# Up-projection by Strassen's products in the later batches, with weight parts kept in DRAM

## The chip, the cores and the metric

The kernel runs on one core of a Trainium2 chip. What counts is the device time of one execution in microseconds; lower is better. The kernel before takes 679.81 us, the median of three runs (679.27 to 683.58). The engines are named as in the profile: PE is TensorE (matmuls; PEld is its weight load), DVE is VectorE, ACT is ScalarE, POOL is GpSimd, and SP is SyncE, whose queue issues every DMA of this kernel in the order in which they are written.

## What is computed

For each of four batches: an attention with eight heads of 64 channels over 768 tokens, where each query sees a band of 31 keys and 24 block summaries, and then a block on the result x (768 tokens x 512 channels).

```python
scores_l = scale * q @ k.T, masked to |i - j| < 16
scores_s = scale * q @ k_sum.T + log(32)      # k_sum: maximum of each block of 32 keys
a = softmax over both
x = a @ [v, v_sum]                            # v_sum: mean of each block of 32 values
...
h = xt @ U @ V                                # mixes the 768 tokens, rank 32
u = x + h.transpose(0, 2, 1)
ch = np.maximum(u @ w_ch1, 0.0) @ w_ch2       # 512 -> 2048 -> 512
out = u + ch
```

U, V and both weights come as 64-bit floats, everything else in 32 bits.

## The kernel before

**Numbers.** A product of two 32-bit matrices is made of three fast matmuls: each operand is split into a high part (rounded) and a low part (the rest), and high x high, high x low and low x high are added in PSUM. `split` makes the parts: ACT rounds, DVE or POOL subtracts.

**The block on x.** `mix_t`, `mix_s` and `mix_u` compute u with channels on the partitions; `mix_u` (L507) puts three transposes of x and one matmul of the mixing into one PSUM bank, and `mix_u_out` splits the result into uh and ul. `up(st, hf, f)` (L567) makes a piece: 128 hidden channels f (16 of them) for one half hf of the tokens (384), as 12 matmuls with the weights loaded into the array and 384 tokens streaming. `up_out` applies the ReLU and splits into gh and gl (ACT L586, DVE L587). `down` (L590) adds a piece to four PSUM accumulators, one for each 128 output channels, 12 matmuls of 384 columns. `down_rows` (L603) does the same with the gates loaded and 512 weight columns streaming, 9 matmuls for a half of the tokens, and leaves tokens on the partitions.

**The first batch.** Its attention is written out by hand in `START`. A loop over f with both halves inside follows (16 columns, each with four places numbered 4f to 4f+3), since the weights are converted in it: `load_weight` brings 512 KB of 64-bit words, `scale_f64` (ACT), `turn_weights` (POOL and DVE) and `split_weights` (ACT and POOL) make the parts. All 32 tiles of parts stay in SBUF for the rest of the kernel. The loads run up to seven columns ahead. The places 13 to 57 also hold the 28 steps of the second batch's attention (`places`). The rows that `down_rows` leaves are turned by 24 transposes (`turn_rows`, L648).

**The later batches.** A list of 32 pieces a batch, first one half of the tokens, then the other: `up` of a piece, `down` of the piece before it, and one step of the next batch's attention (`later_step`). `finish` adds the result to u (held in `outs`) and stores it.

**Order.** Every engine executes its instructions in the order in which they are written, and waits on semaphores in between. The attention of a head goes: `scores` (PE L290), `exponentials` (DVE L310, ACT L320), `turn_squares` (DVE L340, then a store of 384 KB to DRAM), `fetch_squares` (four loads), `square_values` (PE L389), `normalise` (DVE L401 to L403). `key_maxima` (DVE L255, L272) needs the loaded keys, `value_summaries` (ACT L276) writes rows beside the loaded values.

## Time and profile before

| | |
|---|---|
| median of three runs | 679.81 us |
| the profiled execution's own time | 680.63 us |
| its span on the core | 678.8 us |
| mean granted TensorE clock | 0.997 |
| DMA traffic | 78.31 MB, read 61.73 and written 15.73 in HBM |
| largest group of matmuls | L573 (up), 225.4 us busy for uh, 110.6 us for ul |
| second | L595 (down), 210.3 us and 128.3 us |

A row of a group gives the line, engine, operation and tiles, the count after x, the busy time and the mean length of one in ns, and the idle time of the engine ahead of it with what ended that. Matmuls overlap in the array, so the mean length of a matmul is longer than the interval at which they follow each other. Starts in the timeline show that interval.

### The profile page before, as it was taken

How to read it: one execution, taken by the hardware profiler on the slowest of the kernel's cores; microseconds unless marked ns; L12 is line 12 of the kernel's file. 1: busy time of each engine (PE TensorE's matmuls, PEld its weight loads, DVE VectorE, ACT ScalarE, POOL GpSimd, SP SyncE). 2: the span in 40 equal slices, each digit the busy share in tenths (PEclk: the TensorE clock that was granted, in tenths of full speed). 3: DMA queues.
4: the chain of work that ended last, by engine and by line, in shares of the span. 5: the costliest groups of instructions: out<-in, count | busy, mean ns of one | idle time of the engine just before them, and what ended most of it. 6: DMA issues, size and time to landing. Idle time of an engine off the chain costs nothing.

```text
span 678.8 us, 13070 instructions
## 1 busy us (share of the span) xinstructions
PE 655.2 (97%) x5148; PEld 625.4 (92%) x5148; DVE 303.0 (45%) x947; ACT 216.9 (32%) x511; POOL 199.2 (29%) x292
## 2 busy tenths in 40 slices
PE   5889989999999999999999999999999999999997
PEld 4778868888888999999999999999999999999997
DVE  3677687776755544344321444445431221111112
ACT  3855354554622332223321132333321121111110
POOL 5745956955658222100005003020020120000000
PEclk9999998999999999999999999999999999999999
DMA  9999757783252254334234144335210010001001
GB/s 240 239 327 350 248 164 221 224 224 96 74 134 66 97 151 139 112 113 149 66 112 96 46 108 129 113 112 159 79 60 22 8 40 1 1 1 46 1 1 47
DMA packets 65597, 78.31 MB, mean 115 GB/s; under 512 B 5888, under 2 KB 53888, under 8 KB 65536
## 3 DMA queue, kind: packets, MB, share of 16 engines
q1 hardware_dynamic: 65536, 77.49, 39.3%
q8 instruction: 40, 0.66, 0.4%
q14 instruction: 21, 0.17, 0.1%
HBM read 61.73 MB, written 15.73 MB: 114 GB/s over the span
## 4 chain that ended last, share of the span: by engine, by line
PE 78%; POOL 1%; DMA 1%; DVE 1%; SPq 1%; issue 0%; ACT 0%; DVEq 0%
PE ps_h L573 34%; PE acc L595 29%; PE acc L609 5%; PE ps_s L290 4%; PE ps_x L389 3%; PE ps_u L511 1%; DMA at<-there 1%; PE ps_m L477 1%; PE ps_u L519 1%; POOL val L139 0%; PE ps_o L648 0%; PE ps_r L495 0%; POOL ws L164 0%; DVE o L630 0%; DVE squares L340 0%
## 5 line engine op out<-in xcount | busy, mean ns | idle before, releaser
L573 PE MATMUL ps_h<-uh,ws 128*128 128x384 f32 x1024 | 225.4, 341 | 1.4 <-DVE gl L587 1.4
L595 PE MATMUL acc<-gh,ws 128*128 128x384 f32 x768 | 210.3, 334 | 0.0
L573 PEld LDWEIGHTS ps_h<-uh,ws 128*128 128x128 f32 x1024 | 179.4, 189 | 5.9 <-DVE gl L587 2.0
L587 DVE SCALAR_TENSOR_TENSOR gl<-ps_h,gh 128x384 fp32r<-128x384 f32 x128 | 71.3, 557 | 247.0 <-ACT gh L586 246.8
L586 ACT ACTIVATE gh<-ps_h 128x384 fp32r<-128x384 f32 x128 | 63.0, 492 | 273.3 <-PE ps_h L573 273.2
L595 PEld LDWEIGHTS acc<-gh,ws 128*128 128x128 f32 x768 | 140.0, 188 | 0.0
L595 PE MATMUL acc<-gl,ws 128*128 128x384 f32 x384 | 128.3, 334 | 0.0
L573 PE MATMUL ps_h<-ul,ws 128*128 128x384 f32 x512 | 110.6, 336 | 0.5 <-DVE ul L532 0.5
L320 ACT ACTIVATE e<-e,neg 128x120 f32<-128x120 f32 x192 | 61.8, 388 | 111.0 <-DVE neg L310 108.6
L573 PEld LDWEIGHTS ps_h<-ul,ws 128*128 128x128 f32 x512 | 91.7, 189 | 1.3 <-DVE ul L532 1.3
L595 PEld LDWEIGHTS acc<-gl,ws 128*128 128x128 f32 x384 | 72.1, 188 | 0.0
L310 DVE CUSTOM_DVE_ANT_0 e<-ps_s,mask_sb 128x120 f32<-128x120 f32 x192 | 43.8, 279 | 51.8 <-PE ps_s L290 50.8
L609 PE MATMUL acc<-ws,gh 128*128 128x512 f32 x192 | 66.6, 401 | 0.0
L139 POOL TENSOR_SCALAR val<-raw 128x512 f32<-128x512 f32 x29 | 47.8, 1666 | 31.9 <-ACT raw L126 30.4
L305 POOL MEMSET e<- 128x8 f32 x24 | 2.5, 105 | 183.2 <-DVE squares L340 183.1
L623 POOL TENSOR_TENSOR o<-uh,ul 128x384 f32<-128x384 f32 x32 | 32.5, 1041 | 56.4 <-DVE ul L532 48.2
L164 POOL TENSOR_TENSOR ws<-val,ws 128x512 fp32r<-128x512 f32 x29 | 38.7, 1356 | 25.9 <-ACT ws L163 20.9
L230 POOL TENSOR_TENSOR stage<-stage 128x256 f32<-128x256 f32 (+1 forms) x48 | 30.8, 641 | 46.4 <-DMA stage<-in_vn 44.6
L609 PEld LDWEIGHTS acc<-ws,gh 128*128 128x128 f32 x192 | 35.9, 188 | 7.8 <-POOL ws L164 0.5
L290 PEld LDWEIGHTS ps_s<-kt,qz 128*128 128x128 f32 x288 | 38.8, 191 | 2.3 <-DVE kt L272 1.5
L290 PE MATMUL ps_s<-kt,qz 128*128 128x120 f32 x288 | 39.7, 274 | 1.0 <-DVE kt L272 1.0
L609 PE MATMUL acc<-ws,gl 128*128 128x512 f32 x96 | 37.8, 393 | 0.0
(78 smaller groups left out, 557.4 us busy)
## 6 DMA issues: line engine op xcount, KB each, us to landing
raw<-in_w SPq DMA_DIRECT2D x32, 512.0 KB, 7.7
there<-squares SPq DMA_DIRECT2D x24, 384.0 KB, 2.6
at<-there SPq DMA_DIRECT2D x96, 96.0 KB, 2.6
vt<-in_v SPq DMA_DIRECT2D x48, 146.2 KB, 3.6
kt<-in_k SPq DMA_DIRECT2D x24, 288.0 KB, 4.1
stage<-in_vn SPq DMA_DIRECT2D x24, 256.0 KB, 4.6
out_t<-o SPq DMA_DIRECT2D x32, 192.0 KB, 2.0
qz<-in_q SPq DMA_DIRECT2D x28, 128.0 KB, 4.4
```

Of the source, the lines that this page charges most:

```text
L139: nc.gpsimd.tensor_scalar(f32(bits), f32(hi), 0.0, None, ALU.mult)
L164: engine.tensor_tensor(lo, val, f32(hi), ALU.subtract)
L230: nc.gpsimd.tensor_tensor(t[:, :n], t[:, :n], t[:, n : 2 * n], ALU.add)
L290: nc.tensor.matmul(ps[:, i * KC : (i + 1) * KC], qt[:, 64 + j * P : 64 + j * P + P], kt[:, k0 : k0 + KC], start=True, stop=True,)
L310: nc.vector.tensor_tensor_reduce(out=e[:, i, :], in0=ps[:, i * KC : (i + 1) * KC], in1=mask_sb[:, m, :], scale=-SCALE, scalar=BIG, op0=ALU ...
L320: nc.scalar.activation(e[:, i, :], e[:, i, :], AF.Exp, bias=st.neg[h][:, u : u + 1], scale=-1.0,)
L573: nc.tensor.matmul(ps[:, :NH], w_split[0, f][:, part_w, c * P : (c + 1) * P], ut[:, c, :], start=(n == 0), stop=(n == 3 * NC - 1),)
L586: nc.scalar.activation(gh, ps[:, :NH], AF.Relu)
L587: nc.vector.scalar_tensor_tensor(gl, ps[:, :NH], 0.0, f32(gh), ALU.max, ALU.subtract)
L595: nc.tensor.matmul(acc[c][:, :NH], w_split[1, f][:, part_w, sl], gt, start=(first and j == 0), stop=(last and j == 2),)
L609: nc.tensor.matmul(acc[t], gt[:, sl], w_split[1, f][:, part_w], start=(first and j == 0), stop=(last and j == 2),)
L623: nc.gpsimd.tensor_tensor(o, f32(uh)[:, c, :], f32(ul)[:, c, :], ALU.add)
```

## The change

**Up.** In batches 1 to 3 the up-projection of a whole batch is computed by Strassen's scheme. The matrices are cut in two by two: the tokens into halves, the channels c into even and odd chunks of 128, the hidden channels f into pairs. For each of eight pairs p seven products are computed instead of eight. `product` is 6 matmuls of 384 columns (three of parts, two chunks). Two PSUM accumulators, x and y, take several products each, and ACT and DVE carry intermediate sums into a hidden tile in SBUF (`up_phase`). The weight operands are A11, A12, A22 and four sums S1 to S4; the token operands are B11, B21, B22 and four differences T1 to T4 (`operands`).

**Down.** A second phase goes through the 16 hidden tiles by rows: 18 matmuls of 512 columns each, into six accumulators, with the gates of the next tile made ahead (`gates`). The mixing is added to x in rows (`mix_rows`), and the output of a batch is turned by `finish` at the start of the next one; that of the last batch comes at the end.

**Weights.** SBUF now keeps a ring of five places for each weight matrix. In the first batch the parts of both weights are stored to DRAM (`store_weight`), the sums S1 to S4 are made, split and stored (`sum_weights`, `store_sums`), and raw loads run up to four columns ahead. From then on each tile is fetched from DRAM in the order of its use, four tiles for a pair and one for a column of down, into the ten places (`fetch_weight`; `tick` issues a fetch some steps after a place is given back).

**Steps.** The next batch's attention and mixing is now a list of 46 steps (`later_steps`), in the places 13 to 61 of the first batch and 15 of them in the up phase and 31 in the down phase of a later one. A head's squares are sent one step after they are turned, fetched a head later and used two steps after that.

```diff
-    def borrow(i, f):
-        return wt.tile([P, 2 * DM], F32, name="borrowed", tag=f"w{i}_{f}")
+    def weight_place(i, f, dt=F32):
+        return wt.tile([P, 2 * DM], dt, name="place", tag=f"w{i}_{f % RING}")
...
+        if a == 0:
+            if 1 <= h <= H:
+                send_squares(st, h - 1)
+            if 2 <= h <= H + 1:
+                fetch_squares(st, h - 2)
+            if h < H:
+                scores(st, h, 0)
+                exponentials(st, h, 0)
+            if 3 <= h <= H:
+                load_v(st, h - 1)
+        elif a == 1:
+            if h < H:
+                scores(st, h, 1)
+                exponentials(st, h, 1)
+            if h + 1 < H:
                 key_maxima(st, h + 1)
+            if 1 <= h <= H:
+                for t in range(2):
+                    value_summaries(st, h - 1, t, nc.scalar.copy)
+        else:
+            if h + 2 < H:
                 load_qk(st, h + 2)
...
+            if 2 <= h <= H + 1:
+                square_values(st, h - 2)
+                normalise(st, h - 2)
+            if h < H:
+                turn_squares(st, h)
...
+    def mix_rows(st, i, k):
...
+        x = st.x[:, 2 * k : 2 * k + 2, i * 2 * P : (i + 1) * 2 * P]
+        nc.vector.tensor_tensor(x, x, ps.rearrange("p (j c) -> p j c", j=2), ALU.add)
...
+    def operands(st, i, k):
...
+        ps = turn_tokens(st, k < 2, 2 * i + k % 2)
...
+        elif k == 2:
+            part("B11", ps)
+            st.tmp["T2"] = tmp()
+            nc.vector.tensor_tensor(st.tmp["T1"], st.tmp["T1"], ps, ALU.subtract)
+            nc.vector.tensor_tensor(st.tmp["T2"], st.tmp["T3"], ps, ALU.add)
+            part("T1", st.tmp["T1"])
+            part("T2", st.tmp["T2"])
...
+    def sum_weights(p, n):
...
+        if n == 0:
+            nc.vector.tensor_tensor(raw[:, 1], a2[:, 0], a2[:, 1], ALU.add)
+            nc.vector.tensor_tensor(raw[:, 0], raw[:, 1], a1[:, 0], ALU.subtract)
+        else:
+            nc.vector.tensor_tensor(raw[:, 0], a1[:, 0], a2[:, 0], ALU.subtract)
+            nc.vector.tensor_tensor(raw[:, 1], a1[:, 1], w_sums[p, 0][:, 0], ALU.subtract)
...
+        for b in range(2):
+            split(parts[:, b, 0], parts[:, b, 1], raw[:, b], nc.vector if b else nc.gpsimd)
...
+    def fetch_weight():
+        if len(fetched) < len(stream):
+            key = stream[len(fetched)]
+            there = w_there[key]
+            t = weight_place(*first_places[len(fetched) % (2 * RING)], F32R)[:, : there.shape[-1]]
+            nc.sync.dma_start(out=f32(t), in_=there)
...
+    def traffic(f, i):
+        if i == 0:
+            if 0 < f and f + RING - 1 < NF:
+                load_weight(0, f + RING - 1)
+            if f > NF - RING:
+                fetch_weight()
+        if i == 1 and f > 0:
+            store_weight(1, f - 1)
...
+            store_weight(0, f)
+        if i == 3 and f > 0:
+            store_sums((f - 1) // 2, (f - 1) % 2)
...
+        for p in range(NF // 2):
...
+            a11, a12 = use_weight("A", p)
+            x = half_bank("ps_h")
+            product(x, a11, op["B11"], first=True)
+            nc.scalar.copy(c[:, 0, 0], x)
+            yield
+            y = half_bank("ps_h")
+            product(y, a12, op["B21"], first=True)
+            nc.vector.tensor_tensor(c[:, 0, 0], c[:, 0, 0], y, ALU.add)
+            free_place()
+            yield
+            if prev:
+                third(*prev)
+                yield
+            s2, s1 = use_weight("S0", p)
+            product(x, s2, op["T2"])
+            nc.scalar.copy(c[:, 0, 1], x)
+            yield
+            if prev:
+                second(*prev)
+                yield
+            y = half_bank("ps_h")
+            product(y, s1, op["T1"], first=True)
+            free_place()
+            yield
+            s3, s4 = use_weight("S1", p)
+            (a22,) = use_weight("D", p)
+            product(x, s3, op["T3"])
...
+            nc.scalar.copy(c[:, 1, 1], x)
+            nc.vector.tensor_tensor(c[:, 1, 1], c[:, 1, 1], y, ALU.add)
...
+    def down_phase(st, g):
...
+            w = use_weight("down", f)
+            ahead = gates(st, f + 1) if f + 1 < NF else None
...
+    def finish(st, hf, c):
+        ps = turn_tokens(st, hf, c)
+        o = mo.tile([P, DM], F32, name="o", tag="val", bufs=8)[:, :NH]
+        nc.scalar.copy(o, ps)
...
-    pieces = [(b, hf, f, hf * NF + f) for b in range(1, B) for hf in range(2) for f in range(NF)]
...
-            g = up_out(up(cur, hf, f))
...
-            down(acc, pf, pg, pf == 0, pf == NF - 1)
...
+    UP, DOWN = 7 * NF // 2 - 2, NF * NU
+    FIRST_STEPS = 15
...
+        steps = spread(mine, 4, UP)
...
+        steps = spread(theirs, 0, DOWN - 5)
```

How the order of instructions moves shows at three places. First the SP queue in the first batch's loop, where the second batch's attention runs. Before: L540 is a raw weight load, L205 and L206 values, L350 the squares' fetch, L342 their store, L184 to L191 keys and queries.

```order
L205 DMA vt<-in_v 96x390
L206 DMA vt<-in_v 96x390
L350 DMA at<-there 32x4x192 x4
L342 DMA there<-squares 128x768
L184 DMA kt<-in_k 128x3x192
L190 DMA qz_84<-in_q 64x3x128
L191 DMA qz_84<-in_q 64x4x128
L540 DMA raw_1653<-in_w 128x1024
L540 DMA raw_1655<-in_w 128x1024
```

After (L638 raw load, L698 store of parts, L227 and L228 values, L375 fetch, L367 store of squares, L206 to L213 keys and queries):

```order
L367 DMA there<-squares 128x768
L375 DMA at<-there 32x4x192 x4
L227 DMA vt<-in_v 96x390
L228 DMA vt<-in_v 96x390
L638 DMA place<-in_w 128x1024
L698 DMA weight<-place 128x1024 x2
L206 DMA kt<-in_k 128x3x192
L212 DMA qz_83<-in_q 64x3x128
L213 DMA qz_83<-in_q 64x4x128
L638 DMA place<-in_w 128x1024
```

Stores of weight parts stand between the attention's transfers, and the values are loaded later against their use. Second, DVE in the same stage. Before (L145 and L148 convert weights, L340 turns squares, L587 is gl, L401 to L403 normalise):

```order
L340 STREAM_TRANSPOSE squares<-e 128x768
L145 SCALAR_TENSOR_TENSOR val<-raw_780,val 128x512
L587 SCALAR_TENSOR_TENSOR gl<-ps_h,gh 128x384
L145 SCALAR_TENSOR_TENSOR val<-raw_687,val 128x512
L401 TENSOR_SCALAR sum<-ps_x 128x6
L402 RECIPROCAL sum<-sum 128x6
L403 TENSOR_TENSOR x<-ps_x,sum 128x6x64
```

After (L166 is the conversion, L362 turns squares, L758 is gl, L426 to L428 normalise, L685 and L686 make S1 and S2, L185 is a split):

```order
L426 TENSOR_SCALAR sum<-ps_x 128x6
L427 RECIPROCAL sum<-sum 128x6
L428 TENSOR_TENSOR x<-ps_x,sum 128x6x64
L362 STREAM_TRANSPOSE squares<-e 128x768
L685 TENSOR_TENSOR place<-val 128x256
L686 TENSOR_TENSOR place<-place,val 128x256
L185 TENSOR_TENSOR place<-place 128x256
L166 SCALAR_TENSOR_TENSOR val<-place,val 128x512
L758 SCALAR_TENSOR_TENSOR gl<-ps_h,gh 128x384
```

Three operations of 256 columns now stand between the squares and the next gl. Third, the end of PE. Before:

```order
L595 MATMUL acc_6781<-gl,ws_2635 128x384
L595 MATMUL acc_6781<-gh,ws_2635 128x384
L595 MATMUL acc_6782<-gh,ws_2635 128x384
L595 MATMUL acc_6782<-gl,ws_2635 128x384
L595 MATMUL acc_6782<-gh,ws_2635 128x384
```

After (L1108 is down by rows, L592 the transposes of `finish`):

```order
L1108 MATMUL acc_7077<-place,gh 128x512
L1108 MATMUL acc_7081<-place,gh 128x512
L1108 MATMUL acc_7081<-place,gl 128x512
L1108 MATMUL acc_7081<-place,gh 128x512
L592 MATMUL ps_o<-ident_sb,x 128x128 x24
```

The accumulators no longer end the work of PE: 24 transposes follow the last of them.

447 lines of the change are left out of this document (272 added, 175 removed).

## The prediction

> **What bounds the kernel now.** I read the page first: its engine row, the two rows of the span in slices, and the chain.
>
> ```profile
> span 678.8 us, 13070 instructions
> PE 655.2 (97%) x5148; PEld 625.4 (92%) x5148; DVE 303.0 (45%) x947; ACT 216.9 (32%) x511; POOL 199.2 (29%) x292
> PE   5889989999999999999999999999999999999997
> DMA  9999757783252254334234144335210010001001
> PE 78%; POOL 1%; DMA 1%; DVE 1%; SPq 1%; issue 0%; ACT 0%; DVEq 0%
> ```
>
> TensorE is busy for 97% of the span and carries 78% of the chain (what is left of 100% the page's smaller rows take). Only the first three slices (51 us) and the sixth show a TensorE below 9, and in the first three the DMA row stands at 9. So the time is a count of TensorE instructions, and the change is worth what it takes out of that count, minus the waits that it adds. Whether it adds some is a matter of stages, so I asked for busy time by stage: the first batch's loop, the second batch, the last batch, and two short stretches for DMA alone.
>
> ```profile
> 80.00:218.00 138.00, 132.49 (x1083) 117.13 (x1083) 95.82 (x259) 64.18 (x144) 92.84 (x95) 0.99 0.53 149
> 218.00:378.00 160.00, 159.87 (x1346) 156.71 (x1345) 64.66 (x227) 47.22 (x113) 29.83 (x61) 1.00 0.38 110
> 538.00:678.80 140.80, 137.43 (x798) 136.98 (x796) 25.90 (x48) 17.69 (x36) 4.06 (x4) 1.00 0.05 18
> 50.00:58.00 8.00, 7.47 (x47) 6.64 (x47) 7.94 (x16) 6.33 (x14) 3.22 (x2) 1.00 1.03 408
> 300.60:302.60 2.00, 2.00 (x13) 2.00 (x13) 0.00 (x0) 0.34 (x1) 0.00 (x0) 1.00 0.51 197
> ```
>
> The columns are the stretch, its length, then busy us of PE, PEld, DVE, ACT and POOL, the granted clock, the DMA share and GB/s. From 218 us on TensorE has no gap at all, at full clock, and every other engine is below half. In the first batch's loop (80 to 218 us) the other engines are much busier: DVE 69%, POOL 67%, ACT 47%, DMA 53%. That is the stage to which the change adds work.
>
> **What it takes from and gives to TensorE.** TensorE's own timeline has the price of each kind.
>
> ```profile
> 202.79 0.59 PE L495 MATMUL ps_r<-t,rep_sb 128*128 128x256 f32 x2
> 203.03 1.05 PE L573 MATMUL ps_h<-uh,ws 128*128 128x384 f32 x4
> ...
> 210.00 0.39 PE L609 MATMUL acc<-ws,gh 128*128 128x512 f32 x1
> ...
> 212.07 0.49 PE L511 MATMUL ps_u<-ident_sb,x 128*128 128x128 f32 x3
> ...
> 212.58 0.86 PE L573 MATMUL ps_h<-uh,ws 128*128 128x384 f32 x4
> ...
> 219.82 1.48 PE L648 MATMUL ps_o<-ident_sb,r 128*128 128x128 f32 x12
> 221.06 0.94 PE L573 MATMUL ps_h<-uh,ws 128*128 128x384 f32 x4
> ...
> 660.70 0.85 PE L573 MATMUL ps_h<-uh,ws 128*128 128x384 f32 x4
> ...
> 664.86 0.85 PE L573 MATMUL ps_h<-uh,ws 128*128 128x384 f32 x4
> ```
>
> Starts count here, since ends overlap. From 660.70 to 664.86 one piece of 24 matmuls of 384 columns: 173.3 ns each. From 210.00 to 212.07 nine matmuls of 512 columns: 230 ns each. From 212.07 to 212.58 one step of mix_u: 0.51 us. Two matmuls of 256 columns: 0.24 us. Twelve transposes: 1.24 us, 0.103 us each.
>
> - Up: 7 products of 6 matmuls for 8 pairs are 336 a batch, against 384. 48 x 0.1733 = 8.3 us less a batch.
> - Down by rows: 288 x 0.230 = 66.2 us against 384 x 0.1733 = 66.5 us: 0.3 us less. With the line above, three batches give 25.9 us.
> - Mixing: eight mix_u go (4.1 us); six mix_rows come (6 x 0.24 = 1.4 us), 24 transposes for the operands (2.5 us) and 24 more for the output, which now stands in rows (2.5 us). The last batch's output transposes belong to the end, below. Three batches: 4.3 + 7.4 + 5.0 - 12.2 = +4.5 us.
> - The end. Now:
>
> ```profile
> 674.48 1.60 DVE L630 TENSOR_TENSOR o<-o,acc 128x384 f32<-128x384 f32 x3
> 674.54 1.90 SPq L631 DMA_DIRECT2D out_t<-o  x4
> 675.09 0.34 PE L595 MATMUL acc<-gh,ws 128*128 128x384 f32 x1
> ```
>
> The last matmul ends at 675.4 and the span at 678.8, 3.4 us later. After the change one DVE addition, 24 transposes, eight ACT copies and eight stores follow it. ACT is the longest: 8 x 0.48 us (row L364 below) are 3.8, ahead of it three transposes and a hand-over (0.5), behind it the last store as now (its issue ends at 676.4, some 0.4 after it began, so 2.7 from issue to the end). 7.1 against 3.4: +3.7 us.
>
> The sum without any wait: -25.9 + 4.5 + 3.7 = -17.7 us, from 680.6 us (the profiled execution's own time) to 662.9.
>
> **What the first batch's loop gets.** Its 5.5 us of TensorE gaps are in today's time already. These rows price the additions:
>
> ```profile
> L587 DVE SCALAR_TENSOR_TENSOR gl<-ps_h,gh 128x384 fp32r<-128x384 f32 x128 | 71.3, 557 | 247.0 <-ACT gh L586 246.8
> L164 POOL TENSOR_TENSOR ws<-val,ws 128x512 fp32r<-128x512 f32 x29 | 38.7, 1356 | 25.9 <-ACT ws L163 20.9 <-DVE val L145 5.1
> L623 POOL TENSOR_TENSOR o<-uh,ul 128x384 f32<-128x384 f32 x32 | 32.5, 1041 | 56.4 <-DVE ul L532 48.2 <-DMA out_t<-o 8.0
> L145 DVE SCALAR_TENSOR_TENSOR val<-raw,val 128x512 int32<-128x512 int32 x32 | 27.0, 845 | 0.8 <-POOL val L139 0.6
> L403 DVE TENSOR_TENSOR x<-ps_x,sum 128x384 f32<-128x384 f32 x32 | 17.8, 558 | 1.1
> L364 ACT COPY borrowed<-ps_t 120x384 f32<-120x384 f32 x16 | 7.0, 480 | 4.7 <-PE ps_x L375 2.4 <-PE ps_t L358 2.3
> L638 DVE COPY r<-acc 128x512 f32<-128x512 f32 x2 | 1.4, 686 | 1.2 <-DMA out_t<-o 1.2
> ```
>
> - DVE: sum_weights brings six additions of 256 columns for each of eight pairs. 384 columns take 0.558, 512 take 0.686, so 256 about 0.43: 48 x 0.43 = 20.6 us. Operands: 14 x 0.558 = 7.8. mix_rows: 6 x 0.686 = 4.1. Four mix_u_out go (2.2). +30 us on 95.8 in 138: 91%.
> - POOL: 16 halves of a split of 256 columns, about 0.73 us each by the two POOL rows (11.7), eight T splits (8.3), four fewer residuals (-4.2): 92.8 + 15.8, 79%.
> - ACT: 32 casts of 256 columns and 16 operand copies, at most 0.48 each: under 23 us, 63%.
> - DMA: the stores are 8 x 1.835 MB + 16 x 0.524 MB = 23.1 MB, and ten tiles (4.7 MB) are fetched ahead. Loads in 4 KB rows moved 408 GB/s at a share of 1.03, and the store of squares 197 GB/s at 0.51, so 386 at a full share. 59.8 + 11.6 = 71 us on 0.53 x 138 = 73: 144 us in 138.
>
> So DMA is over its capacity in that stage and DVE is near it. The Trainium skill, DMA: Bandwidth & Descriptors (Specifications), limits one core's traffic with HBM to about 358 GB/s; by that the 27.8 MB would take 78 us, not 71, and the forecast below would be 681. The trace speaks against it for loads, with 408; for stores and loads mixed no row tells.
>
> It is worse in the middle. The attention of the next batch had 28 steps over 46 places; now 46 steps lie over 50 places, its 32 attention steps first. Columns f = 4 to 8 now hold six heads' rounds. TensorE there: 5 x (24 x 0.1733 + 18 x 0.230) = 41.5, and of the 26.9 us by which the second batch's 160 us exceed 32 x 4.16, some 2.3 us a head remain after the mixing: 55 us in all. DMA: ten raw loads (12.8), the stores of five columns (7.2 MB, 18.7), and six heads; the second batch's 61 us of DMA for 17.6 MB, without 3.7 MB of outputs and value rows, make 6.0 us a head (36), and two value-row loads 3.6. 71 us for 55. The SP queue is in order and each transfer waits behind the stores, so this lag reaches the consumers: key_maxima (DVE) comes two steps after its load, value_summaries (ACT) one step after load_v, and gl or gh of the running pieces stand behind them on these engines. What hides part of it is the lead of the raw loads, one column or more (11 us). Bounds: nothing, if the lag stays inside the leads, and 16 us, if none does. I take 8, the middle, since the raw loads have a lead and the attention's loads hardly any.
>
> START loses four raw loads (2.1 MB, 5 us of queue). They stood last in its queue, so I count 0; at best -2.
>
> **What the up phases wait for.** Each of 32 tiles comes through a ring of ten places.
>
> ```profile
> raw<-in_w SPq DMA_DIRECT2D x32, 512.0 KB, 7.7
> vt<-in_v SPq DMA_DIRECT2D x48, 146.2 KB, 3.6
> ...
> raw<-in_w SPq DMA_DIRECT2D x16, 512.0 KB, 9.0
> borrowed<-in_v SPq DMA_DIRECT2D x8, 292.5 KB, 10.3
> ```
>
> The first two rows are medians to landing over the whole span, the last two over its first 60 us, when the DMA share was full. The tightest place is that of S1: freed by `second` in the next pair, fetched three ticks on, and needed as A seven ticks after that. A tick is 6 x 0.1733 = 1.04 us, and 0.7 head a pair adds 1.6 us: a lead of 8.9 us. A pair's DMA is 1.835 MB (4.5 us) and 0.7 head (4.2), 8.7 us in a period of 8.9, so the queue runs nearly full and landings lie between 7.7 and 10.3 us. Bounds: 0, and 1.4 us in each of eight pairs of two batches, 22 us. Nearest is the overall median, which is inside the lead: I take 2 us for each of these two batches. The last batch has no attention beside it.
>
> On ACT a copy of a product may stand behind three exponentials that wait for DVE. The same accumulator is written again two products (2.08 us) after, and the copy takes 0.48: 1.6 us of cover. In the down phase gates(f+1) has a whole column of 18 x 0.230 = 4.1 us. I cost both at nothing; without cover it would be under 1 us a head.
>
> **Forecast.** 662.9 + 8 + 4 = 674.9 in the terms of the profiled 680.6, which stands 0.8 above the median of 679.8. So 674.
>
> **Rivals.**
> - Absorbed: the lag stays inside the leads and the ring never runs dry. For it: the DMA row falls to 5 in the sixth slice (85 to 102 us), just ahead of the dense columns, and TensorE's gaps of 5.5 us can take some. Time: 662.9 + 2 - 0.8, about 664. Chance 0.23.
> - The first batch pays in full. DVE needs 59 us in the dense columns (six heads of 4.75, by the second batch's 64.7 us less 32 gl and sixteen operations of 0.558; ten gl; twenty conversions at 0.845; eighteen sums) against TensorE's 55, beside a DMA queue that needs 71. In L145, whose two inputs both lie in SBUF, the mean is 0.845, though 512 columns take 0.686 in L638; the sums are of that kind. DVE, ACT and DMA wait for each other in turn, so no lead hides anything: 16 us instead of 8, 682. Against it: the 5 in the sixth slice. The Trainium skill, SBUF — State Buffer (Who interferes with whom), says that a DVE instruction with two SBUF inputs and a GpSimd instruction that reads SBUF block each other; the trace agrees, in that L403, with one input in PSUM, keeps to 558 ns. The page on DMA cited above would bring the first batch to about the same 681. Chance 0.14.
> - Slower: tiles come late. At the full queue's 10.3 us to landing, S1's place is late by 1.4 us in every pair of batches 1 and 2, 22 us instead of 4: 692. It decides from a landing of about 9.9 us on (1.0 us late in each of 16 pairs). For it: the queue is full by the count; against: tiles in 4 KB rows landed faster than v's short rows. Chance 0.18.
>
> The forecast itself has 0.45, with 667 to 681 as its own range.
>
> **How the numbers follow.** A measurement of this kernel can tell about 1%: faster is below 673.0, slower above 686.6. Of the forecast's 0.45 I put 0.20 below 673 and the rest within; the absorbed case is faster; the full lag 0.10 within and 0.04 slower; the late tiles 0.02 within and 0.16 slower. Faster 0.43, same 0.37, slower 0.20. The range from 661 to 691 leaves out the far end of the last rival (0.1) and a little below.
>
> **What would show it.** Up: 336 matmuls of 384 columns a later batch at about 173 ns from start to start; down: 288 at 230 ns. First batch: DMA share near 1 between 95 and 160 us and TensorE's gaps there on ACT gh or DVE gl, with kt or vt loads behind them. Up phases: waits of TensorE for a place's DMA show the late tiles. If the first batch ends by 222 us, the absorbed case holds; if a later batch takes more than 160 us, the late tiles do. I am wrong if TensorE's start-to-start intervals differ, or if the end takes more than 8 us.

## The result, and the profile after

The changed kernel takes 710.13 us (median of 4 runs, 704.8 to 710.82); the kernel before took 680.44 beside it (median of 4, 679.27 to 683.58). The ratio is 1.041, with a 95% interval from 1.035 to 1.047: 4% slower, where 674 had been forecast, and above the range of 661 to 691. The profiled execution took 709.69 us, 707.9 of them in the span.

The head of the page of the changed kernel:

```profile
span 707.9 us, 13102 instructions
...
PE 653.6 (92%) x4800; PEld 577.8 (82%) x4800; DVE 382.0 (54%) x1057; ACT 283.0 (40%) x639; POOL 203.6 (29%) x300
...
PE   5898797989899889899799999899799999999997
...
PEclk9999999999999999999899999999899999999999
DMA  9999779999789859999757449999854338775102
...
PE 50%; DMA 12%; SPq 1%; DVE 1%; issue 1%; ACT 0%; ACTq 0%
```

TensorE has 348 instructions fewer (4800 for 5148) and is busy for only 1.6 us less (653.6 for 655.2). Its share of the chain fell from 78% to 50%, and 12% are now DMA. The granted clock shows an 8 in two slices. The DMA row, which had faded to between 1 and 5 in the second batch, stays at 5 or more in most slices of the first three.

By stage: the span is cut where a batch's first up product starts, so the rows are start, first batch, second, third, and fourth with the end. The columns are those of the prediction's stretches. After:

```profile
0.00:51.60 51.60, 39.48 (x456) 34.04 (x457) 33.46 (x160) 30.83 (x89) 30.50 (x76) 0.97 1.01 288
51.60:243.20 191.60, 171.52 (x1255) 147.72 (x1253) 147.78 (x355) 93.36 (x213) 128.13 (x134) 0.97 0.89 291
243.20:410.30 167.10, 156.12 (x1207) 138.64 (x1205) 87.19 (x258) 60.62 (x134) 26.73 (x56) 0.97 0.79 244
410.30:573.90 163.60, 157.19 (x1217) 140.00 (x1216) 79.43 (x239) 62.89 (x140) 18.27 (x36) 0.97 0.73 227
573.90:707.90 134.00, 129.25 (x673) 117.37 (x671) 34.15 (x49) 35.27 (x64) 0.00 (x0) 1.00 0.47 165
```

Before, cut in the same way:

```profile
0.00:53.20 53.20, 39.14 (x456) 33.93 (x457) 33.87 (x160) 31.17 (x89) 30.61 (x76) 1.00 1.02 274
53.20:221.10 167.90, 161.87 (x1234) 143.20 (x1233) 116.43 (x291) 77.39 (x169) 117.42 (x122) 0.99 0.60 176
221.10:379.30 158.20, 158.06 (x1335) 155.31 (x1333) 64.02 (x228) 45.81 (x110) 27.17 (x55) 1.00 0.38 111
379.30:538.00 158.70, 158.66 (x1333) 155.98 (x1333) 62.74 (x223) 44.81 (x108) 19.91 (x36) 1.00 0.30 89
538.00:678.80 140.80, 137.43 (x798) 136.98 (x796) 25.90 (x48) 17.69 (x36) 4.06 (x4) 1.00 0.05 18
```

The first batch grew by 23.7 us and the two middle ones by 8.9 and 4.9. Only the last batch, which has no attention beside it, became shorter, by 6.8.

TensorE's idle time in a stage is the length less PE busy. But busy time hides something: a matmul at half clock counts as busy for nearly twice as long (behind 343 us matmuls of 512 columns start every 0.43 us, at full clock every 0.23). The trace also records when the granted clock was at half, in pieces of 3.41 or 6.83 us, 34.1 us in all in the changed kernel. Of these 4.3 us lie in gaps, where there is no work to slow; of the 29.9 us in which PE is busy, I count half as lost. That makes a ledger in us, before -> after:

| stage | length | TensorE idle | lost to the clock | rest: work at full clock |
|---|---|---|---|---|
| start | 53.2 -> 51.6 | 14.1 -> 12.1 | 0 -> 1.7 | 39.1 -> 37.8 |
| first batch | 167.9 -> 191.6 | 6.0 -> 20.1 | 1.7 -> 5.1 | 160.2 -> 166.4 |
| second | 158.2 -> 167.1 | 0.1 -> 11.0 | 0 -> 3.9 | 158.1 -> 152.2 |
| third | 158.7 -> 163.6 | 0.0 -> 6.4 | 0 -> 4.2 | 158.7 -> 153.0 |
| fourth, end | 140.8 -> 134.0 | 3.4 -> 4.7 | 0 -> 0 | 137.4 -> 129.3 |
| sum | 678.8 -> 707.9 | 23.6 -> 54.3 | 1.7 -> 14.9 | 653.5 -> 638.6 |

So the work fell by 14.8 us, of the 18.9 that the prediction counted; 30.7 us of waiting and 13.2 us of lowered clock ate it up. What TensorE waits for (line, releaser, us in total, times, longest) in the first batch of the changed kernel, the three largest:

```profile
PE ps_x L414 <- DMA at<-there: 4.6, 2, 2.8
PE acc L767 <- POOL place L185: 4.0, 5, 1.6
PE ps_s L312 <- DVE kt L294: 2.3, 2, 2.0
```

and in its second and third batch together, all but one of 1.0 us:

```profile
PE ps_x L414 <- DMA at<-there: 10.0, 3, 4.6
PE ps_x L414 <- DMA vt<-in_v: 4.4, 1, 4.4
PE ps_h L1011 <- ACT place L1071: 2.0, 1, 2.0
```

In the first batch the waits are small and of all kinds: by the whole list 18 on VectorE, GpSimd and ScalarE, 14.4 us in all and none over 2.0, beside three on DMA with 5.4. In the middle batches they are few and long, and not one is for a weight tile: TensorE waits for the attention's squares and values, which stand in the same queue. The squares of the third batch's head 3, in the chain of waits:

```profile
320.21 6.20 DMA at<-there
...
326.43 8.38 DMA qz<-in_q
...
334.82 6.60 DMA at<-there
...
341.66 0.40 PE ps_x L414 x5
```

Three landings of 6 to 8 us, each issue released by the one before, end in a wait of 4.6 us. This wait and the 4.4 us for values lie in the down phases, each some 18 us after the first down matmul; the two shorter waits for squares (3.4 and 2.0) lie in the up phases. Landing times say the same. After (median us at the end of a row):

```profile
place<-weight SPq DMA_DIRECT2D x120, 512.0 KB, 5.2
...
there<-squares SPq DMA_DIRECT2D x24, 384.0 KB, 6.7
at<-there SPq DMA_DIRECT2D x96, 96.0 KB, 5.0
```

Before:

```profile
there<-squares SPq DMA_DIRECT2D x24, 384.0 KB, 2.6
at<-there SPq DMA_DIRECT2D x96, 96.0 KB, 2.6
```

A round trip of a head's squares through DRAM went from 5.2 to 11.7 us by these medians.

### The profile page after: what moved, and what is told of

Read it like the earlier page. It is cut to its first block, busy times and chain, and to the rows that moved or that the text cites. A ratio compares the mean times of both kernels' runs of the same rounds, so it can differ in the third digit from the quotient of the medians.

```text
span 707.9 us, 13102 instructions
## 1 busy us (share of the span) xinstructions
PE 653.6 (92%) x4800; PEld 577.8 (82%) x4800; DVE 382.0 (54%) x1057; ACT 283.0 (40%) x639; POOL 203.6 (29%) x300
## 4 chain that ended last, share of the span: by engine, by line
PE 50%; DMA 12%; SPq 1%; DVE 1%; issue 1%; ACT 0%; ACTq 0%
PE acc L1108 26%; PE ps_h L1011 18%; DMA at<-there 4%; DMA stage<-in_vn 2%; DMA place<-weight 2%; PE ps_x L414 2%; PE ps_s L312 2%; PE ps_o L592 2%; DMA qz<-in_q 1%; DMA there<-squares 1%; DMA vt<-in_v 1%; PE ps_u L583 0%; DVE squares L362 0%; SPq L213 0%; SPq L375 0%
## 5 line engine op out<-in xcount | busy, mean ns | idle before, releaser
L1108 PE MATMUL acc<-place,gh 128*128 128x512 f32 x576 | 195.5, 403 | 0.0
L1011 PE MATMUL ps_h<-op,place 128*128 128x384 f32 x1008 | 190.8, 342 | 2.0 <-ACT place L1071 2.0
L1011 PEld LDWEIGHTS ps_h<-op,place 128*128 128x128 f32 x1008 | 176.4, 191 | 3.7 <-ACT place L1071 2.3
L1108 PEld LDWEIGHTS acc<-place,gh 128*128 128x128 f32 x576 | 109.6, 190 | 23.5 <-issue 1.1
L1108 PE MATMUL acc<-place,gl 128*128 128x512 f32 x288 | 113.5, 394 | 0.0
L1093 DVE SCALAR_TENSOR_TENSOR gl<-place,gh 128x768 fp32r<-128x768 f32 x48 | 48.2, 1005 | 76.1 <-ACT gh L1092 76.1
L745 PE MATMUL ps_h<-place 128*128 128x384 f32 x384 | 77.4, 351 | 1.2 <-DVE place L574 0.5
L342 ACT ACTIVATE e<-e,neg 128x120 f32<-128x120 f32 x144 | 46.5, 386 | 75.1 <-DVE neg L332 74.2
L745 PEld LDWEIGHTS ps_h<-place 128*128 128x128 f32 x384 | 69.9, 196 | 4.5 <-DVE place L574 1.3
L767 PE MATMUL acc<-place,gh 128*128 128x512 f32 x192 | 68.5, 412 | 4.4 <-POOL place L185 4.0
L1108 PEld LDWEIGHTS acc<-place,gl 128*128 128x128 f32 x288 | 55.1, 191 | 9.7
L185 POOL TENSOR_TENSOR op<-tmp,op 128x384 fp32r<-128x384 f32 x24 | 24.4, 1030 | 108.9 <-ACT op L184 108.8
L160 POOL TENSOR_SCALAR val<-place 128x512 f32<-128x512 f32 (+1 forms) x30 | 47.9, 1613 | 19.7 <-DMA stage<-in_vn 11.7
L767 PEld LDWEIGHTS acc<-place,gh 128*128 128x128 f32 x192 | 36.3, 191 | 14.2 <-POOL place L185 6.2
L185 POOL TENSOR_TENSOR place<-val,place 128x512 fp32r<-128x512 f32 x29 | 39.4, 1380 | 16.7 <-ACT place L184 16.7
L414 PEld LDWEIGHTS ps_x<-vt,at 120*32 120x32 f32 x1152 | 19.1, 116 | 27.8 <-issue 12.2
L414 PE MATMUL ps_x<-vt,at 120*32 120x65 f32 x1152 | 23.0, 231 | 19.9 <-DMA at<-there 14.7
```

Source lines behind the costliest of these rows:

```text
L160: nc.gpsimd.tensor_scalar(f32(bits), f32(hi), 0.0, None, ALU.mult)
L185: engine.tensor_tensor(lo, val, f32(hi), ALU.subtract)
L342: nc.scalar.activation(e[:, i, :], e[:, i, :], AF.Exp, bias=st.neg[h][:, u : u + 1], scale=-1.0,)
L414: nc.tensor.matmul(ps[32 * i : 32 * i + 32, u * DV : (u + 1) * DV], at[:KC, i, u], vt[u % 2][:, (u // 2) * 2 + (i // 2 + u) % 2], start=Tr ...
L745: nc.tensor.matmul(ps[:, :NH], w_split[0, f][:, c % 2, part_w, c // 2], ut[:, c, :], start=(n == 0), stop=(n == 3 * NC - 1),)
L767: nc.tensor.matmul(acc[t], gt[:, sl], w_split[1, f][:, part_w], start=(first and j == 0), stop=(last and j == 2),)
```

## The experiments

Times are medians, with the kernel before measured beside each and the ratio to it. "The first loop" is the first batch's stage above. Five kernels run it unchanged, and their profiled executions took 191.6, 189.8, 189.8, 188.6 and 189.8 us: mean 189.9, so differences of 2 us mean nothing there.

**1. A third of the bytes.** Of each tile only some columns are stored and fetched; the products read them again in place of the others.

```
-        nc.sync.dma_start(out=t, in_=f32(src))
+        n = 512 if key[0] == "down" else 256
+        nc.sync.dma_start(out=t[:, :n], in_=f32(src)[:, :n])
...
-            nc.sync.dma_start(out=f32(t), in_=there)
+            nc.sync.dma_start(out=f32(t)[:, :n], in_=there[:, :n])
```

> Of every stored and fetched weight tile only a part of the columns moves (256 of 1024 of the tiles of the up product, 512 of 1024 of the down tiles; about 36% of the bytes), the same transfers in the same order; the products read the columns that are there twice or four times, so the output is wrong and the arithmetic is the same. Theory 1 (bytes: the stores and fetches fill the DMA engines, and the attention's own loads land behind them): the first batch's loop falls from 195 us to about 170, the two middle batches from 163 to about 156 each, sum 52 + 170 + 2 x 156 + 134 = 668, between 662 and 676. Theory 2 (the sums' arithmetic on VectorE and GpSimd holds up the first batch): the first loop stays at 190 or more and only the middle batches gain, 52 + 192 + 2 x 156 + 134 = 690, between 685 and 697. Theory 3 (the number of transfers on one queue and their order, whatever their size): no change, 703 to 712.

686.69 us (684.03 to 689.81), ratio 1.011 (1.008 to 1.014). The stages of the first three batches:

```profile
52.30:239.70 187.40, 168.82 (x1255) 144.51 (x1253) 147.06 (x355) 93.31 (x213) 129.31 (x134) 0.99 0.71 210
239.70:395.00 155.30, 152.14 (x1206) 135.40 (x1205) 87.05 (x258) 60.49 (x134) 26.79 (x56) 1.00 0.55 162
395.00:548.30 153.30, 153.30 (x1218) 136.71 (x1218) 78.64 (x239) 62.84 (x140) 18.24 (x36) 1.00 0.49 147
```

Theory 2 of that text comes nearest: the middle batches fall to 155.3 and 153.3, the third without a single gap, while the first loop keeps 187.4 with its DMA share down from 0.89 to 0.71. Bytes explain the middle batches, and of the first loop at most some 2.5 us, hardly more than the spread. Theory 3, the number of transfers and their order, falls.

**2. Five stores instead of 56,** later fetches of full size from the first tile of each kind.

```
+        if key[1] == 0:
             t = dram.tile(list(src.shape), F32, name="weight", ...)
             nc.sync.dma_start(out=t, in_=f32(src))
+            w_there[key] = t
+        w_there[key] = w_there[key[0], 0]
```

> Only the first tile of each kind is stored (5 stores instead of 56), and every later fetch reads that one, at full size; the weights of the later batches are then wrong. Theory 1 (bytes): the first loop loses some 21 MB and goes from 195 us to about 172, the middle batches stay at 163: 52 + 172 + 2 x 163 + 134 = 684, between 678 and 692. Theory 2 (sums' arithmetic): the first loop stays near 190, 700 to 710. Theory 3 (number and order on the queue): the first loop gains as in theory 1, but so it would not in the run with a third of the bytes.

705.76 us, ratio 1.034 (1.027 to 1.041). First loop 187.0, middle batches 166.5 and 163.4, as in the changed kernel. The prediction counted 59.8 us of DMA for 23.1 MB of stores; leaving out 21 MB of them gains the first loop some 3 us, in one execution. This was the larger part of the DMA argument for that stage, and it is nearly all hidden.

**3. Full stores, a third of the fetches.**

> The stores are whole, and only the fetches of the later batches move part of the columns (256 of 1024, down 512 of 1024); the output of the later batches is wrong. Theory 1 (bytes): the first loop stays at about 192, the middle batches go to 156: 52 + 192 + 2 x 156 + 134 = 690, between 685 and 697. Theory 3: no change, 703 to 712. With the two runs before it this splits the loss into the part of the stores and the part of the fetches; if bytes alone count, the two gains add up to that of the run with a third of all bytes, within 5 us.

689.82 us, ratio 1.011 (1.003 to 1.018). First loop 189.8; middle batches 156.9 and 153.3. As theory 1 said, within its numbers: the fetches make the middle batches' loss. The squares' fetches landed in 3.0 us there (median of the two batches) against 5.7 in the changed kernel.

**4. Without the sums.** Four places are filled once and stored at the sums' points; no addition, no split.

```
-        if n == 0:
-            nc.vector.tensor_tensor(raw[:, 1], a2[:, 0], a2[:, 1], ALU.add)
...
-        for b in range(2):
-            split(parts[:, b, 0], parts[:, b, 1], raw[:, b], nc.vector if b else nc.gpsimd)
+        w_sums[p, n, "parts"] = sum_places[p % 2, n]
```

> The sums of the weights are not formed in the first batch (24 additions and subtractions and 32 splits of 128 x 256 on VectorE, ScalarE and GpSimd left out; four places are filled once and stored at the same points, so the traffic is the same); the later batches' output is wrong. Theory 1 (bytes): VectorE had 91% in the loop by plan, so a little comes back, 0 to 6 us: 704 to 710. Theory 2 (sums' arithmetic): the first loop falls from 195 us to about 172, 682 to 692.

697.26 us, ratio 1.022 (1.013 to 1.030). First loop 177.7, 12.2 under the mean of the unchanged ones: between the two theories, and nearer to the second. TensorE's waits in that loop, the two largest:

```profile
PE ps_x L414 <- DMA at<-there: 6.1, 3, 2.7
PE ps_x L414 <- DVE val L166: 1.1, 1, 1.1
```

The waits for VectorE and GpSimd have shrunk, the one for squares has grown. The edit takes work off three engines at once (busy time in that loop falls by 28.2 us on VectorE, 13.6 on GpSimd and 7.4 on ScalarE), so it does not tell which of them held TensorE up. The sums' own prices in the changed kernel, VectorE's rows grouped by line and shape (the split of 128x256, L185, first):

```profile
L185 DVE TENSOR_TENSOR place<-place 128x256 fp32r<-128x256 f32 x16 | 11.2, 699 | 13.0 <-ACT place L184 13.0
...
L685 DVE TENSOR_TENSOR place<-val 128x256 f32<-128x256 f32 x8 | 5.5, 688 | 0.0
L686 DVE TENSOR_TENSOR place<-place,val 128x256 f32<-128x256 f32 x8 | 5.4, 670 | 0.3
...
L688 DVE TENSOR_TENSOR place<-val 128x256 f32<-128x256 f32 x8 | 4.4, 550 | 0.0
...
L689 DVE TENSOR_TENSOR place<-val,place 128x256 f32<-128x256 f32 x8 | 3.9, 482 | 0.0
```

30.4 us for the 48 operations, 0.63 us each; some of their times overlap, and without them VectorE is busy for 28.2 us less, 0.59 each.

**5. Both: no sums and a third of the bytes.**

> Both at once: the sums of the weights are not formed in the first batch, and stored and fetched tiles move only part of their columns (256 of 1024, down 512 of 1024); the later batches' output is wrong. Theory A (two causes that stand in for each other in the first loop: a late DMA landing where VectorE is not late, VectorE where the DMA is not): the first loop, 191.6 us in the changed kernel, 187.3 with a third of the bytes and 177.7 without the sums, falls to about 170; with the middle batches as with a third of the bytes, 155.4 and 153.3, the sum is 52.5 + 170 + 155.4 + 153.3 + 134 = 665, between 661 and 670. Theory B (the loop's order on TensorE itself, with the mixing's rows and the turns of tokens in it, is what costs): the loop stays above 175, the time above 671.

671.6 us (670.05 and 673.14), ratio 0.984 (0.979 to 0.989), and the first loop at 173.0: the time is just above theory A's window, the loop below B's bound of 175. The gains do not stand in for each other, they add: 2.5 + 12.2 = 14.7 from the two single edits, 16.9 together. This also bounds what these two causes can give back: with a third of the bytes and no sums the kernel, which then computes something else, is 1.6% faster than before.

**6. Waits filled with products that nobody reads.**

```
         ps = st.psx[h] = bank("ps_x")
+        for _ in range({0: 10, 3: 18}.get(h, 0) if st.b > 1 else 0):
+            nc.tensor.matmul(ps[:, :NH], vm_st[:, :P], vm_st[:, :NH], start=True, stop=True)
```

> Ahead of the product of squares and values of heads 0 and 3 of the third and fourth batch, the four places where TensorE waited 3.4, 4.6, 2.0 and 4.4 us, stand products that nobody reads (10 of 128x128 by 128x384 for head 0, 18 for head 3, some 1.7 and 3.1 us); the output stays right. Theory A (a wait of about 2 us or more halves the TensorE clock for 3.4 or 6.8 us behind it): the granted clock no longer falls at these places, 3.4 + 6.8 + 3.4 + 6.8 us at half clock go, some 6.6 us of which lay behind the waits: 702 to 706. Theory B (the clock falls for another reason, or the time is given back at the next DMA wait): 708 to 713.

703.14 us (698.59 to 707.08), ratio 1.030 (1.025 to 1.036) against 1.041 (1.035 to 1.047); the intervals just touch. 56 more matmuls, 9.7 us of work at 0.173 us, and the median is 1% lower. What they do is to be seen in the 3 us behind two of the long waits. The changed kernel (columns as above; the clock stands after the five engines):

```profile
341.70:344.70 3.00, 3.00 (x52) 2.54 (x53) 1.38 (x4) 0.00 (x0) 0.00 (x0) 0.50 0.66 253
...
505.00:508.00 3.00, 2.99 (x52) 2.54 (x53) 1.33 (x4) 0.00 (x0) 0.00 (x0) 0.50 0.56 216
```

With the waits filled:

```profile
340.10:343.10 3.00, 3.00 (x58) 2.52 (x59) 2.11 (x5) 0.00 (x0) 0.07 (x1) 1.00 0.66 258
...
504.70:507.70 3.00, 2.98 (x57) 2.54 (x58) 1.98 (x5) 0.00 (x0) 0.05 (x1) 1.00 0.73 268
```

PE is busy for all of the 3 us in both. Only the clock, 0.50 and 1.00, tells them apart. Theory A's number holds, and at the four places no half clock is left (the 3.41 us at 260.8 stood behind another wait, for ScalarE, and stayed). But the gain that can be put down to it is small: in the profiled executions the two middle batches take 328.5 us instead of 330.7. There the added work fills 6.1 us of idle time and saves 6.4 us of clock; the rest of the difference in the medians lies elsewhere or in the spread.

**7. Nine attention steps in the up phases instead of 15.**

```
-    FIRST_STEPS = 15
+    FIRST_STEPS = 9
```

> In the up phases of the middle batches 9 steps of the next batch's attention instead of 15, the other 6 in the down phases, where the DMA engines were busy 45 to 60% instead of 91 to 93%. Theory A (the up phases of the middle batches are filled by the weights' and the attention's bytes together): the waits on the attention's loads shrink from 11 + 6.4 us idle and 10 us of lowered clock by half, 697 to 704. Theory B (latency of the chain send, fetch, product, whatever the load): 707 to 712; a denser down phase may also turn the wait over to VectorE, 712 to 718.

701.23 us (698.92 to 701.97), ratio 1.026 (1.023 to 1.030); middle batches 161.4 and 162.1. The second batch gets back 5.7 us, the third 1.5. The two waits in the up phases are gone. Those in the down phases stay, now some 15 us after the first down matmul; they are longer, 4.7 and 5.8 us, and both for squares:

```profile
PE ps_x L414 <- DMA at<-there: 11.3, 3, 5.8
```

11.3 us for squares, where it was 10.0, though without the wait for values. TensorE's idle time in the two batches falls from 17.4 to 12.5 us, not by half. So theory A holds in its time and direction: how the traffic is spread matters. The medians of squares' landings fell to 4.2 us out and 3.0 back, so what is left is in single bursts, which a median does not show.

**8. Plain fp32 values in DRAM,** half the bytes; after each fetch ScalarE and GpSimd divide a tile in its place. The first batch then need not divide the sums.

```
+            nc.sync.dma_start(out=f32(t)[:, n : 2 * n], in_=there)
...
+    def divide(upto):
+        while len(divided) < min(upto, len(fetched)):
+            t = fetched[len(divided)][1]
+            nc.scalar.copy(t[:, 0], f32(t)[:, 1])
+            nc.gpsimd.tensor_tensor(t[:, 1], f32(t)[:, 1], f32(t)[:, 0], ALU.subtract)
+            divided.append(t)
...
+        divide(len(used) + 2)
```

> The tiles are stored and fetched as plain fp32 values, half the bytes, and divided into their two parts after each fetch (ScalarE copy and GpSimd subtraction of 128x512, 40 a batch); the sums are then not divided in the first batch (32 copies and 32 subtractions of 128x256 less there). The output stays right. Theory A (bytes and the first batch's arithmetic together): the first loop goes to about 178, the middle batches to about 156 and 154: 52.5 + 178 + 156 + 154 + 134 = 674.5, between 669 and 682, faster than the kernel before. Theory B (the division behind each fetch comes late, ScalarE and GpSimd wait for landings and hold up the gates): above 690.

715.47 us (714.42 to 719.14), ratio 1.049 (1.045 to 1.053): theory B. TensorE's waits in the first three batches:

```profile
PE ps_h L1024 <- POOL place L736: 11.1, 11, 4.9
PE ps_h L1024 <- ACT place L735: 8.0, 7, 1.9
PE acc L780 <- POOL place L185: 6.6, 3, 5.1
```

L735 and L736 are the division: late, as theory B had it. The third row is another new wait: behind that split GpSimd had waited 4.8 us for a value buffer that a store still read. Half the bytes, and new waits that cost more: the first loop took 186.3 us, the middle batches 172.3 and 165.5. Beside the divisions VectorE's gl of 768 columns rose from 1005 to 1240 ns. The Trainium skill, SBUF — State Buffer (Who interferes with whom), says that a VectorE instruction with two SBUF inputs and a GpSimd instruction that reads SBUF hold each other up; this row agrees.

**9. The same, stored a round earlier and divided four tiles ahead of use.**

```
-        divide(len(used) + 2)
+        divide(len(used) + 4)
...
-            store_weight(0, f)
+            if f + 1 < NF:
+                store_weight(0, f + 1)
```

> As the kernel with plain fp32 values in DRAM, but each value tile is stored in the round it is ready (a round earlier for the up weights), and a fetched tile is divided four tiles ahead of its use instead of two, the first ones before the first batch ends; the output stays right. Theory A (that kernel lost its gain to its own new waits: value buffers held by the stores, 5.1 and 6.5 us in the first loop with 6.8 us of lowered clock, and divisions that came late, 4.9 us and more in the up phases): the first loop goes from 186 us to about 170, the up phases from 86 and 80 to 72 and 70: 53 + 170 + 72 + 86 + 70 + 86 + 59.5 + 75.5 = 672, between 666 and 680, faster than the kernel before. Theory B (the divisions themselves load ScalarE and GpSimd too much): the up phases stay above 76 and the time above 690.

687.99 us (686.77 to 691.75), ratio 1.010 (1.004 to 1.017): 27 us less than the version before, yet above theory A's 680. First loop 177.2, middle batches 164.5 and 155.8. One wait of 5.8 us was left at the start of the second batch: ScalarE's copy of the finished rows stood 9.2 us behind GpSimd's value sums, for a shared buffer, and the first product's copy stood behind it.

**10. Nine steps on top of it.**

> The same with 9 instead of 15 attention steps in the up phases of the middle batches. Theory A: with half the bytes the DMA engines have room in both phases, so that it makes little difference, within 3 us of the run beside it; if the divisions still come late in the up phases, the emptier up phases gain 2 to 5 us more.

699.69 us, ratio 1.027 (1.020 to 1.033), middle batches 169.1 and 163.3. Worse by 1.7%, against both guesses: the setting that helped at full bytes costs here. Perhaps it is since the down phases now carry divisions too; that was not tried.

**11. The buffer of that wait:** eight divisions on VectorE, two of three row tiles in the gates' buffers.

```
+            lower = nc.vector if len(divided) < 8 else nc.gpsimd
...
+                r = f32(gate_place(("gh", "gl")[t - 1]))[:, :DM]
```

> As the last kernel but one (plain fp32 values in DRAM, stored early, 15 steps), with the first eight divisions on VectorE instead of GpSimd and two of the three row tiles that leave the first batch in the gates' buffers instead of the shared value buffers. Theory A (the one wait of 5.8 us at the start of the second batch came from a row copy that waited for a value buffer, which GpSimd's sums held because the divisions went before them): that wait and the 3.4 us of lowered clock behind it shrink to under 2 us: 688 - 4 - 3 = 681, between 677 and 685. Theory B (something else holds the first products): the wait stays, 686 to 690.

682.48 us (680.15 to 684.91), ratio 1.002 (1.000 to 1.005): theory A, though the two edits were not tried apart. The wait is gone, the middle batches take 156.9 and 157.3, the mean clock is 0.996. This is the best version with the right output, and it is no faster than the kernel before.

**12. Six waits of known length** in the last batch's up phase, which ran for 59.0 us without a gap.

```
+            if st.b == B - 1 and p in WAITS:
+                idle = mo.tile([P, DM], F32R, name="idle", tag="val", bufs=VALS)[:, :NH]
+                nc.scalar.copy(idle, x)
+                for _ in range(WAITS[p] - 1):
+                    nc.scalar.copy(idle, f32(idle))
+                nc.tensor.matmul(bank("ps_idle")[:, :NH], vm_st[:, :P], idle, start=True, stop=True)
```

> The changed kernel with six added waits in the up phase of the last batch, where TensorE ran without a gap: behind pairs 1 to 6 a product waits for a chain of 1, 2, 3, 4, 5 and 7 ScalarE copies that begins when the product before is done, so that TensorE should stand idle for some 1.2, 1.7, 2.2, 2.6, 3.1 and 4.1 us; nobody reads the added products. Theory A (a wait of about 2 us or more lowers the granted clock behind it, a shorter one does not): the up phase grows from 59 us by the idle time, about 15 us, and by some 1.7 us more for each of the three or four longer waits: 59 + 15 + 6 = 80, and the clock's records show half speed behind the longer waits alone. Theory B (the clock falls for other reasons): 59 + 15 = 74 and no half speed there.

731.65 us, ratio 1.074 (1.068 to 1.081). The six gaps were 0.95, 1.49, 2.03, 2.58, 3.12 and 4.21 us. The 3 us behind the last five, and the phase as a whole:

```profile
599.00:602.00 3.00, 3.00 (x17) 3.00 (x18) 0.35 (x1) 0.48 (x1) 0.00 (x0) 1.00 0.97 369
608.80:611.80 3.00, 3.00 (x17) 3.00 (x18) 0.39 (x1) 0.48 (x1) 0.00 (x0) 1.00 0.71 266
619.10:622.10 3.00, 3.00 (x9) 3.00 (x10) 0.00 (x0) 0.37 (x1) 0.00 (x0) 0.51 0.51 202
631.30:634.30 3.00, 3.00 (x12) 3.00 (x13) 0.00 (x0) 0.48 (x1) 0.00 (x0) 0.67 0.37 143
644.80:647.80 3.00, 3.00 (x9) 3.00 (x10) 0.00 (x0) 0.37 (x1) 0.00 (x0) 0.50 0.15 53
573.30:654.40 81.10, 66.72 (x355) 64.50 (x355) 14.60 (x26) 28.93 (x61) 0.00 (x0) 0.92 0.51 177
```

Behind gaps of 1.49 and 2.03 us, 17 matmuls at full clock; behind 2.58 and 4.21, nine in the same time. By the ledger's count 81.1 us = 61.2 of work + 14.4 idle + 5.5 of clock, against theory A's 80; the six added products and the tails of the matmuls ahead of the gaps are in the work. Here the three waits of 2.58 us and more cost clock time on top of their length, the three shorter ones did not.

**13 and 14. What is left of the first loop** in the eleventh version (177.3 us with 12 idle, against 167.9 before the change).

```
-            nc.vector.tensor_tensor(raw[:, 0], a1[:, 0], a2[:, 0], ALU.subtract)
-            nc.vector.tensor_tensor(raw[:, 1], a1[:, 1], w_sums[p, 0][:, 0], ALU.subtract)
+            nc.gpsimd.tensor_tensor(raw[:, 0], a1[:, 0], a2[:, 0], ALU.subtract)
+            nc.gpsimd.tensor_tensor(raw[:, 1], a1[:, 1], w_sums[p, 0][:, 0], ALU.subtract)
```

> As the last kernel with plain values, with two of the four additions and subtractions of each pair's sums on GpSimd instead of VectorE (16 of 128x256, some 11 us of VectorE's 143 in the first loop); the output stays right. Theory A (VectorE's arithmetic sets what is left): the loop goes from 177.4 to about 173 us, 682.5 - 4 = 678, between 675 and 681. Theory B (the stores' bytes): the loop stays at 177, 681 to 684; GpSimd, which had the weights' splits late 3.1 us in four waits, may make it 1 to 3 us longer.

The other leaves out 51 of the 56 stores.

> The same kernel as two before with plain values, with only the first tile of each kind stored (5 stores instead of 56; the later batches' weights are wrong). Theory A: the loop stays above 175, 680 to 683. Theory B: the loop goes to about 171, 674 to 678.

Sums on GpSimd: 686.59 us, ratio 1.007 (1.004 to 1.009), first loop 182.0. VectorE's busy time in the loop fell by 7 us and the loop became longer; GpSimd was no place for them. Without the stores: 678.12 us, ratio 0.994 (0.991 to 0.997), first loop 173.6. So theory B, just above its 678: at half the bytes the stores cost some 3.7 us, about as much as at full bytes. Even with them free, the gain is 0.6%.

## Why the prediction was wrong

**Nearly right: TensorE's work.** Its terms were -25.9, +4.5 and, in the end's share, 2.5 us of transposes: -18.9 us of work. The ledger's last column says -14.8. The later batches bear it out: in run 1 the third batch, without a gap and at full clock, takes 153.3 us, and the ledger has 153.0. What is missing is mostly in the first loop, where the work rose by 6.2 us (by 2.9 in run 5, which has fewer waits); why is not worked out. In the last batch 222 matmuls of the up products run from 594.31 to 632.90, 173.8 ns each, and matmuls of the down phase start every 227 ns (173.3 and 230 in the prediction). The end was put at 7.1 us and took 7.4:

```profile
700.14 0.39 PE L1108 MATMUL acc<-place,gh 128*128 128x512 f32 x1
...
700.37 2.78 PE L592 MATMUL ps_o<-ident_sb,x 128*128 128x128 f32 x24
700.90 3.16 ACT L1124 COPY o<-ps_o 128x384 f32<-128x384 f32 x8 [7.64 <-PE ps_o L592]
```

From 700.5, where the last matmul of the down phase ends, to 707.9.

**Wrong: "Bounds: nothing [...] and 16 us [...] I take 8", for the first batch's loop.** It got 23.7 us longer, 14.1 of it in idle time. The error lies in what was put on the path. The step went by the DMA queue, 71 us of transfers for 55 of TensorE; but without the stores only about 3 us come back, without the sums 12. So the failed step is the path, and the sums' weight on it. The sums stood on the list, at 0.43 us each, scaled from a copy with one input and operations that read PSUM; they took 0.59 to 0.63, so 28 to 30 us for 20.6. That price alone is not the error: VectorE's busy time in the stage grew by 31.4 us (116.4 to 147.8), close to the +30 that was added up, since other operations took less (the copies into kt 288 ns instead of 385) and some times overlap. The error is that such a load was put at nothing, outside of the DMA lag, as long as VectorE's total stays below TensorE's. In the longer loop VectorE was 77% busy and GpSimd 67%, and yet 18 waits of TensorE on them and ScalarE, 14.4 us, appeared where before there were four, of 2.9 us. The engines work in the order in which the program is written, so what TensorE needs (kt, the normalised x, the mixing, the mask, weight parts from GpSimd) stands behind whatever came first, and a count of busy time does not show it. Which of the three engines carries how much of the 12 us is not shown. Of the prediction's signs a DMA share near 1 between 95 and 160 us did come (0.97), but it was not what cost most of the time. The rival "the first batch pays in full" named DVE, ACT and DMA waiting in turn, and its 16 us were still too few.

**Wrong: "I take 2 us for each of these two batches".** The second and third batch lost 17.4 us idle and 8.1 to the clock. The count that the queue runs nearly full in the up phases (8.7 us of DMA in a period of 8.9) was right: the DMA share from 243.2 to 326 us was 0.91, and with a third of the fetched bytes nearly all of the loss is gone. Its victim was not. I asked only whether the weights' tiles make their lead of 8.9 us; they landed in 5.2 and TensorE never waited for one. The attention's squares, which go out and come back in the same queue with about two steps to spare, waited behind them, and so did the values of one head. Nor was it the up phases alone: 9.0 of the 17.4 us are the two waits in the down phases, for whose DMA the prediction had no term. The rival "tiles come late" has about the right size for these batches (22 us) and the wrong transfer. Its sign, a later batch of over 160 us, did show; the waits for a place's DMA did not.

**Missing: the clock.** No term of the sum had it, and it cost 13.2 us more than before. The trace of before holds one case, a wait of 3.0 us with half clock for 3.41 us behind it; in the stage's row it is the 0.99, and the prediction passed over it.

**The sum again.** From 662.9, the sum without any wait, to the profiled 709.7 it is 46.8 us: 4.1 of work that did not go (14.8 for 18.9), 29.5 of idle time beyond the 1.2 at the end that the sum had (where +12 was taken), and 13.2 of clock.

What stays open: why the waits of the first loop sum up to just 20 us is not derived from anything; the two edits that shorten it add up to 16.9 of the 22 us by which it is longer than before, and the rest, some 5 us, is partly TensorE's own work (163.1 us in the fifth run, 160.2 before).

## What to carry to other kernels

Before trading TensorE instructions for traffic, list every transfer that shares the queue with the new one, and ask of each how many microseconds lie between its issue and its use; here the ones with little slack paid, not the ones that were added. A wait of TensorE beyond some 2 us can cost up to 1.7 or 3.4 us on top of its length (half of a record of 3.41 or 6.83 us; the table below says how often), so read the granted clock beside busy time, which counts slow matmuls as work. Halving the bytes, and with them the sums' splits, gained 28 us of 710, but only after each of its new waits (a buffer, a late conversion) had been found in the list of waits and taken out.

## What the runs showed of the hardware

**The granted clock falls at waits well under 3 us.** In the traces of all sixteen kernels, TensorE's gaps between the start's end and the last 10 us, and at how many a record of half clock began, between the gap's start and 4 us after its end:

| gap, us | gaps | with half clock |
|---|---|---|
| 0.8 to 1.2 | 45 | 2 |
| 1.2 to 1.6 | 43 | 1 |
| 1.6 to 2.0 | 30 | 8 |
| 2.0 to 2.4 | 14 | 5 |
| 2.4 to 3.0 | 11 | 8 |
| over 3.0 | 27 | 23 |

The records have lengths of 3.41 or 6.83 us, whatever the gap. At the gaps over 1.6 us they begin 1.9 to 5.2 us after the gap's start, at 18 of the 23 over 3.0 us before its end; so part of a record can fall into the gap and cost nothing. The known waits show that the gaps are the cause: in a phase that ran at full clock without them, 2.03 us left the clock alone and 2.58 halved it. Each length was tried once there, and the table shows that no sharp limit follows from that. The Trainium skill, TensorE: Matmul & The Clock Gate (HAM oscillation — how this bites in real kernels), gives the rule "no PE-idle gaps >~3.4µs"; the runs put the limit lower, since 13 of 25 gaps between 2.0 and 3.0 us already had half clock. The window of about 3.4 us that the same page describes (What's actually happening) agrees with the length of the records. That it runs free of the kernel, as the Trainium skill says there, would explain why gaps of one length sometimes lower the clock and sometimes do not; no run here was made to show it.

**Added work can cost nothing.** The 56 added matmuls of the sixth run, 9.7 us of work, made the two middle batches 2.2 us shorter, not longer, in the profiled execution: they stood in waits that were there anyway and kept the clock up behind them.
